# Attention with a gated MLP on one core: centred rows for the first gate/up tile by tile, the last transposes between two filler pairs, and the final adds on GpSimd

## The chip, the cores and the metric

One core of one Trainium2 chip. The metric is device time in microseconds (us), median of several executions. TensorE's granted clock in them was 0.999 or 1.0 on average.

## The reference

```python
x  = A_x                                   # 2048 x 512, bf16
xn = _layernorm(x)                         # (x - mean) / sqrt(var + 1e-5), no weight
s  = attention(xn, k_cache, v_cache, wq, wo)   # 32 heads of 128, 2048 keys, output 512 wide
gate, up = xn @ W_gate, xn @ W_up          # 512 -> 1792
y  = ((gate * (gate > 0)) * up) @ W_down   # 1792 -> 512
return x + s * silu(y)
```

The MLP has no bias, and its gate is a ReLU. If a row of xn is written as r·xc, with the centred row xc = x − mean and r = 1/sqrt(var + eps), then gate and up each carry a factor r, ReLU keeps a positive factor, and y carries r². So y can be computed from the centred rows, and r² be put in at the end. This is what the change uses.

## The kernel before

The program runs the MLP in four quarters of 512 rows, then the attention. Three stretches matter.

The head: four row tiles of 128 rows arrive by DMA, are normalized in two pairs, transposed by TensorE and copied to `xnT`. TensorE meanwhile runs 12 + 3 matmuls on zeros (`warm`). They are there for its clock: in the profile they begin 0.43 us apart and, from about 4.2 us on, 0.22 us apart; below, this is called the release of the clock. The first three of the 14 chunks of gate/up then run in two halves of 256 rows.

```python
def head_ln():
    st = ln_stats(0)
    st = ln_stats(1)
    sq01 = ln_aggr([0, 1], st)             # aggregate, then sqrt on ScalarE
    st = ln_stats(2)
    c01 = ln_coef([0, 1], sq01)            # reciprocal, -mean*rstd
    n0 = ln_norm(dve, sem_ln4, 0, c01)
    n1 = ln_norm(dve, sem_ln4, 1, c01)
    head_transpose(0, n0, act, sem_xa)
    head_transpose(1, n1, act, sem_xa)
    warm_mm(3)
    # ... the same for tiles 2 and 3, between
    emit_half(0, range(HFC - 1), xt_ready[0][0:2])   # gate/up, 256 columns
    emit_half(0, range(HFC - 1, HFC), [])
    emit_half(1, range(HFC), xt_ready[0][2:4])
```

Gate/up results go through a ring of three PSUM slots of two banks. A slot is free again once ScalarE's ReLU and VectorE's multiply have read it.

The tail: the last head group's output projection, 16 row tiles. Tiles 0 to 7 run inside the last attention blocks. Tiles 8 to 11 are fillers that TensorE runs while VectorE normalizes the last attention block; then come that block's transposes, then tiles 12 to 15.

```python
def emit_final_tile(n, bank):
    # ... four matmuls into ps_r[:, bank]
    mtok = sem_opa.sig(
        dve.tensor_tensor(fin_tmp[fb][:], ps_r[:, bank, 0:D], g_sb[:, n, :], ALU.mult))
    _wait(dve, mtok)
    ftok = sem_opa.sig(
        dve.tensor_tensor(x_sb[:, n, :], x_sb[:, n, :], fin_tmp[fb][:], ALU.add))
    # ... store: tiles 12 to 15 one by one, the others in pairs

for n in range(NT - 8, NT - 4, 2):
    emit_M([(emit_final_tile, n), (emit_final_tile, n + 1)])
flush_last_transposes()
for n in range(NT - 4, NT, 2):
    emit_M([(emit_final_tile, n), (emit_final_tile, n + 1)])
```

The softmax here doesn't subtract the row's maximum and nothing guards it: scores larger than these inputs give would overflow.

## Time and profile before

| | before |
|---|---|
| time, median | 1288.09 us (1287.98 to 1288.51) |
| span of the profiled run | 1285.8 us |
| TensorE busy | 1279.2 us |
| first gate/up matmul | 7.80 us |
| last P·V matmul ends (as modelled) | 1274.21 us |
| last add ends | 1283.79 us |

From the page of the kernel before, parts 1 and 4 (busy time with share of the span and number of instructions; the chain that ended last, by engine):

```profile
PE 1279.2 (99%) x11995; PEld 834.8 (65%) x11995; DVE 380.0 (30%) x682; ACT 1001.4 (78%) x1109; POOL 10.0 (1%) x21
...
PE 99%; DVE 1%; issue 0%; DMA 0%; ACT 0%
```

The execution that was profiled took 1287.70 us.

TensorE (PE) bounds everything but two ends. From the timeline of its first 14 us (start, length in us, engine, line, operation; in brackets the idle time before it and what ended it):

```profile
1.19 4.25 PE L365 MATMUL ps_r<-warm 128*128 128x512 bf16 x12 [1.19 <-DVE warm L235]
6.16 0.63 PE L353 MATMUL ps_acc<-ident,xn_sb 128*128 128x128 bf16 x8 [0.71 <-DVE xn_sb L340]
...
7.80 0.60 PE L407 MATMUL ps_r<-xnT,Wg_sb 128*128 128x256 bf16 x4 [0.36 <-ACT xnT L359]
...
13.48 1.03 PE L481 MATMUL ps_r<-xnT,Wg_sb 128*128 128x512 bf16 x4
```

From 7.80 us on no bracket stands any more: TensorE is fed without a gap. The other end, from the timeline of the last 14 us:

```profile
1274.04 3.62 PE L759 MATMUL ps_r<-Wo_sb,OT_store 128*128 128x512 bf16 x16
...
1278.33 3.61 PE L759 MATMUL ps_r<-Wo_sb,OT_store 128*128 128x512 bf16 x16 [0.44 <-ACT OT_store L699]
...
1275.21 0.68 DVE L767 TENSOR_TENSOR fin_tmp<-ps_r,g_sb 128x512 bf16<-128x512 f32 x1
1275.93 0.42 DVE L772 TENSOR_TENSOR x_sb<-x_sb,fin_tmp 128x512 bf16<-128x512 bf16 x1
...
1282.64 0.68 DVE L767 TENSOR_TENSOR fin_tmp<-ps_r,g_sb 128x512 bf16<-128x512 f32 x1
1283.36 0.43 DVE L772 TENSOR_TENSOR x_sb<-x_sb,fin_tmp 128x512 bf16<-128x512 bf16 x1
```

VectorE works through eight tiles at (1282.64 − 1275.21)/7 = 1.06 us each, without a gap between 1275.21 and 1283.79, and is 2 us behind TensorE at the end.

### The profile page before, as it was taken

The numbers are of one execution on the slowest core, as the hardware profiler recorded it, in microseconds if no ns is written. First come the engines' busy times: TensorE is split into PE (matmuls) and PEld (weight loads), VectorE is DVE, ScalarE is ACT, GpSimd is POOL, SyncE is SP. The second block draws the span as 40 slices with busy tenths as digits, with TensorE's granted clock in tenths as the row PEclk, the third lists the DMA queues.
The fourth block names the chain that finished last, engine by engine and source line by source line (L and its number), as shares of the span: only waits on it lengthen the run. The fifth ranks groups of instructions, "written<-read, shape, count | busy, mean of one in ns | idle before, by whom it ended". The sixth has DMA issues, their size and how long they took to land.

```text
span 1285.8 us, 26847 instructions
## 1 busy us (share of the span) xinstructions
PE 1279.2 (99%) x11995; PEld 834.8 (65%) x11995; DVE 380.0 (30%) x682; ACT 1001.4 (78%) x1109; POOL 10.0 (1%) x21
## 2 busy tenths in 40 slices
PE   9999999999999999999999999999999999999998
PEld 4444476666666666666666666666666666666665
DVE  6333311112222222222222222222222222234456
ACT  3322399998888888888888888888888888888884
POOL 2000000000000000000000000000000000000000
PEclk9999999999999999999999999999999999999999
DMA  9500123232222332232322322332223321233302
GB/s 266 111 1 1 21 36 67 57 54 40 36 51 50 71 54 50 54 71 51 54 46 37 60 47 53 55 67 55 54 51 71 55 34 38 50 67 55 50 14 74
DMA packets 238801, 71.60 MB, mean 56 GB/s; under 512 B 225632, under 2 KB 238688, under 8 KB 238688
## 3 DMA queue, kind: packets, MB, share of 16 engines
q1 hardware_dynamic: 238400, 69.63, 27.8%
q8 instruction: 96, 1.57, 0.5%
q10 hardware_dynamic: 288, 0.26, 0.1%
q14 instruction: 17, 0.14, 0.0%
HBM read 32.77 MB, written 2.10 MB: 27 GB/s over the span
## 4 chain that ended last, share of the span: by engine, by line
PE 99%; DVE 1%; issue 0%; DMA 0%; ACT 0%
PE ps_acc L722 36%; PE ps_r L625 34%; PE ps_r L558 9%; PE ps_r L579 8%; PE ps_acc L504 4%; PE ps_r L485 4%; PE ps_r L481 4%; PE ps_r L759 1%; DVE fin_tmp L767 0%; PE ps_r L407 0%; DMA x_sb<-in_A_x_dram 0%; DVE stats L315 0%; ACT xnT L359 0%; PE ps_acc L353 0%; DVE x_sb L772 0%
## 5 line engine op out<-in xcount | busy, mean ns | idle before, releaser
L635 ACT ACTIVATE PT<-ps_r 128x1024 bf16<-128x1024 f32 x1024 | 952.5, 1054 | 167.7 <-PE ps_r L625 167.7
L722 PEld LDWEIGHTS ps_acc<-V_sb,PT 128*128 128x128 bf16 x8192 | 621.1, 98 | 241.7 <-ACT PT L635 3.5
L722 PE MATMUL ps_acc<-V_sb,PT 128*128 128x129 bf16 x8192 | 776.5, 220 | 0.0
L625 PE MATMUL ps_r<-QT_sb,KT_sb 128*128 128x512 bf16 x2048 | 754.1, 379 | 0.0
L652 DVE RECIPROCAL rz_sb<-ps_acc 128x4 f32<-128x4 f32 x127 | 23.3, 183 | 729.6 <-PE ps_acc L722 729.6
L625 PEld LDWEIGHTS ps_r<-QT_sb,KT_sb 128*128 128x128 bf16 x2048 | 195.0, 98 | 1.1 <-DVE QT_sb L569 0.4
L558 PE MATMUL ps_r<-xnT,Wq_sb 128*128 128x512 bf16 x512 | 130.9, 379 | 0.0
L579 PE MATMUL ps_r<-Wo_sb,OT_store 128*128 128x512 bf16 x448 | 114.6, 379 | 0.0
L569 DVE CAST QT_sb<-ps_r 128x512 bf16<-128x512 f32 x128 | 88.5, 692 | 48.1 <-PE ps_r L558 48.1
L558 PEld LDWEIGHTS ps_r<-xnT,Wq_sb 128*128 128x128 bf16 x512 | 49.9, 97 | 60.7 <-ACT PT L635 27.1
L655 DVE TENSOR_TENSOR Onorm<-ps_acc,rz_sb 128x512 bf16<-128x512 f32 x127 | 87.8, 691 | 4.4
L579 PEld LDWEIGHTS ps_r<-Wo_sb,OT_store 128*128 128x128 bf16 x448 | 43.8, 98 | 52.9 <-ACT PT L635 0.2
L448 ACT ACTIVATE gr_sb<-ps_r 128x512 bf16<-128x512 f32 x56 | 33.3, 596 | 51.5 <-PE ps_r L481 49.9
L592 DVE TENSOR_TENSOR s_acc<-s_acc,ps_r 128x512 f32<-128x512 f32 x96 | 66.0, 687 | 17.3 <-PE ps_r L579 17.3
L485 PE MATMUL ps_r<-xnT,Wu_sb 128*128 128x512 bf16 x212 | 54.4, 379 | 0.0
L481 PE MATMUL ps_r<-xnT,Wg_sb 128*128 128x512 bf16 x212 | 54.4, 379 | 0.0
L454 DVE TENSOR_TENSOR hT<-gr_sb,ps_r 128x512 bf16<-128x512 bf16 x56 | 38.4, 686 | 46.3 <-PE ps_r L485 42.0
L504 PE MATMUL ps_acc<-Wd_sb,hT 128*128 128x512 bf16 x224 | 49.0, 379 | 0.0
L510 ACT ACTIVATE sig_sb<-ps_acc 128x512 f32<-128x512 f32 x16 | 9.6, 597 | 38.8 <-PE ps_acc L504 38.8
L504 PEld LDWEIGHTS ps_acc<-Wd_sb,hT 128*128 128x128 bf16 x224 | 21.9, 98 | 26.4
L485 PEld LDWEIGHTS ps_r<-xnT,Wu_sb 128*128 128x128 bf16 x212 | 20.7, 98 | 25.0
L481 PEld LDWEIGHTS ps_r<-xnT,Wg_sb 128*128 128x128 bf16 x212 | 20.8, 98 | 24.8
(42 smaller groups left out, 138.7 us busy)
## 6 DMA issues: line engine op xcount, KB each, us to landing
V_sb<-in_A_v_cache_dram SPq DMA_DIRECT2D x32, 512.0 KB, 4.5
Wq_sb<-in_A_wq_dram SPq DMA_DIRECT2D x32, 128.0 KB, 2.4
Wo_sb<-in_A_wo_dram SPq DMA_DIRECT2D x8, 512.0 KB, 3.9
OT_store<-Onorm SPq DMA_TRANSPOSE x127, 2.4
Wd_sb<-in_B_W_down_dram SPq DMA_DIRECT2D x1, 1792.0 KB, 13.6
x_sb<-in_A_x_dram SPq DMA_DIRECT2D x3, 512.0 KB, 10.1
out_dram<-x_sb SPq DMA_DIRECT2D x6, 256.0 KB, 2.2
Wg_sb<-in_B_W_gate_dram SPq DMA_DIRECT2D x1, 768.0 KB, 9.8
```

The costliest lines, as they stand in the source:

```text
L454: dve.tensor_tensor(hT[par][:, fc, :], gr_sb[gk][:], ps_r[:, gb + 1, :], ALU.mult)
L481: ins = pe.matmul(ps_r[:, gb, :], Wg_sb[:, c, fs], xnT[:, c, qs], start=(c == 0), stop=(c == DC - 1))
L485: ins = pe.matmul(ps_r[:, gb + 1, :], Wu_sb[:, c, fs], xnT[:, c, qs], start=(c == 0), stop=(c == DC - 1))
L504: ins = pe.matmul(ps_acc[:, jb, 0:D], hT[par][:, fc, j * 128:(j + 1) * 128], Wd_sb[:, fc, :], start=(fc == 0), stop=(fc == FC - 1))
L558: ins = pe.matmul(ps_r[:, bank, :], Wq_sb[b][:, c, :], xnT[:, c, qs], start=(c == 0), stop=(c == DC - 1))
L569: etok = sem_qpe.sig(dve.tensor_copy(QT_sb[b][:, qs], ps_r[:, bank, :]))
L579: ins = pe.matmul(ps_r[:, bank, 0:D], OT_store[g % 2][:, hh, n * 128:(n + 1) * 128], Wo_sb[g % 2][:, hh, :], start=(hh == 0), stop=(hh == ...
L592: dve.tensor_tensor(s_acc[:, n, :], s_acc[:, n, :], ps_r[:, bank, 0:D], ALU.add)
L625: ins = pe.matmul(ps_r[:, 2 * s + tt, :], KT_sb[h % 2][:, t * 128:(t + 1) * 128], QT_sb[h % 2][:, qs], start=True, stop=True)
L635: act.activation(PT[pb][:], ps_r[:, 2 * s:2 * s + 2, :], ACTF.Exp, scale=scale)
L655: dve.tensor_tensor(Onorm[ob][:], o_ap, rz_sb[:].to_broadcast([128, 4, Dh]), ALU.mult))
L722: ins = pe.matmul(o_ap, PT[pb][:, tt, j * 128:(j + 1) * 128], V_sb[vb][:, t, 0:VW], start=(t == 0 and j % 2 == 0), stop=(t == KT - 1 and j ...
```

## The change

The intent has two parts. Head: start the first gate/up matmuls on centred rows, tile by tile, so that no square root, reciprocal or partner tile stands in front; issue the first weights earlier and on two queues; put r² into the first quarter's SiLU. Tail: run the last transposes after the first filler pair, so that TensorE does not wait for their copies; let GpSimd do the final adds except the last, so that VectorE has only the multiply.

```diff
                 load_x0(sp, 0)
                 load_x0(act, 1)
+                load_w(sp, Wg_sb, wg_src, sem_wg, 0)
+                load_w(act, Wu_sb, wu_src, sem_wu, 0)
                 load_x0(sp, 2)
                 load_x0(act, 3)
-                load_w(sp, Wg_sb, wg_src, sem_wg, 0)
-                load_w(sp, Wu_sb, wu_src, sem_wu, 0)
@@ head, new
+                def head_center(n):
+                    atok = ln_aggr([n], ln_stats(n))
+                    _wait(dve, atok)
+                    return sem_ln4.sig(
+                        dve.tensor_scalar(xc_sb[:, n, :], x_sb[:, n, :], mv[:, n, 0:1], None, op0=ALU.subtract))
                 def head_ln():
+                    ctok = {0: head_transpose(0, head_center(0))}
+                    warm_mm(2)
+                    for n in range(4):
+                        if n + 1 < 4:
+                            ntok = head_center(n + 1)
+                        _wait(pe, ctok[n])
+                        head_tile(n, 0)                    # chunk 0, 128 columns
+                        if n + 1 < 4:
+                            ctok[n + 1] = head_transpose(n + 1, ntok)
+                        for fc in range(1, HFC):
+                            head_tile(n, fc)
@@ cut: the first quarter's norm moves to GpSimd and a DMA transpose, for the Q projection;
@@ its down stage gets r2 (tanh scale, one more VectorE pass per tile)
-                warm_mm(12)
+                warm_mm(10)
@@ tail
-                fin_tmp = [S_([128, D], BF16, "fin_tmp") for _ in range(2)]
+                fin_tmp = [S_([128, D], BF16, "fin_tmp") for _ in range(4)]
-                    _wait(dve, mtok)
+                    eng, sem = (dve, sem_opa) if n == NT - 1 else (pool, sem_xp)
+                    _wait(eng, mtok)
-                    ftok = sem_opa.sig(
-                        dve.tensor_tensor(x_sb[:, n, :], x_sb[:, n, :], fin_tmp[fb][:], ALU.add))
+                    ftok = sem.sig(
+                        eng.tensor_tensor(x_sb[:, n, :], x_sb[:, n, :], fin_tmp[fb][:], ALU.add))
                 for n in range(NT - 8, NT - 4, 2):
                     emit_M([(emit_final_tile, n), (emit_final_tile, n + 1)])
-                flush_last_transposes()
+                    if n == NT - 8:
+                        flush_last_transposes()
```

More of the change, by code (lines that the diff above doesn't have):

```diff
@@ L141, in bass_recurrent_scan__mha_block_cached__glu_gated_reglu__prompt_kernel @@
         xn_sb = SB_([128, NT, D], BF16, "xn_sb")
+        xc_sb = SB_([128, 4, D], BF16, "xc_sb")
+        xcT = SB_([128, DC, NQ], BF16, "xcT")
+        r2 = SB_([128, 4, 1], F32, "r2")
+        r2h = SB_([128, 4, 1], F32, "r2h")
         stats = SB_([128, NT, 6], F32, "stats")
@@ L320, in ln_aggr, with ln_sqrt @@
                         atok = sem_ln2.sig(dve.bn_aggr(mv[:, n, :], stats[:, n, :]))
+                    return atok
+                def ln_sqrt(ns, atok):
                     a, b_ = ns[0], ns[-1] + 1
                     _wait(act, atok)
-                    if a == 0:
-                        _wait(act, warm_tok)
                     return sem_sq.sig(
@@ L343, in _, with head_transpose @@
                 xt_ready = {Q: [] for Q in range(QB)}
-                def head_transpose(n, ntok, eng, sem):
+                def head_center(n):
[3 more added lines that the diff above has]
+                        dve.tensor_scalar(xc_sb[:, n, :], x_sb[:, n, :], mv[:, n, 0:1], None, op0=ALU.subtract))
+                def head_transpose(n, ntok):
                     tp_ps = acc_bf[n % 2]
@@ L353, in head_transpose @@
                         ins = pe.transpose(tp_ps[:, c * 128:(c + 1) * 128],
-                                           xn_sb[:, n, c * 128:(c + 1) * 128], ident[:])
+                                           xc_sb[:, n, c * 128:(c + 1) * 128], ident[:])
                     ptok = sem_tp.sig(ins)
                     src = tp_ps[:, 0:DC * 128].rearrange("p (c q) -> p c q", c=DC)
-                    _wait(eng, ptok)
-                    copy = act.copy if eng is act else dve.tensor_copy
-                    ctok = sem.sig(copy(xnT[:, :, n * 128:(n + 1) * 128], src))
-                    xt_ready[0].append(ctok)
-                    acc_free[n % 2] = ctok
+                    _wait(act, ptok)
+                    acc_free[n % 2] = sem_xa.sig(act.copy(xcT[:, :, n * 128:(n + 1) * 128], src))
+                    return acc_free[n % 2]
                 def warm_mm(k):
@@ L367, in head_ln @@
                 def head_ln():
-                    st = ln_stats(0)
-                    st = ln_stats(1)
-                    sq01 = ln_aggr([0, 1], st)
-                    st = ln_stats(2)
-                    c01 = ln_coef([0, 1], sq01)
-                    n0 = ln_norm(dve, sem_ln4, 0, c01)
-                    n1 = ln_norm(dve, sem_ln4, 1, c01)
-                    head_transpose(0, n0, act, sem_xa)
-                    head_transpose(1, n1, act, sem_xa)
-                    warm_mm(3)
-                    st = ln_stats(3)
@@ L379, in head_ln @@
-                    sq23 = ln_aggr([2, 3], st)
-                    emit_half(0, range(HFC - 1), xt_ready[0][0:2])
-                    c23 = ln_coef([2, 3], sq23)
-                    n2 = ln_norm(dve, sem_ln4, 2, c23)
-                    n3 = ln_norm(dve, sem_ln4, 3, c23)
-                    head_transpose(2, n2, act, sem_xa)
-                    head_transpose(3, n3, dve, sem_xt)
-                    emit_half(0, range(HFC - 1, HFC), [])
-                    emit_half(1, range(HFC), xt_ready[0][2:4])
@@ L389, in _ @@
-                half_slots = []
-                def emit_half(k, fcs, toks):
-                    hs = slice(k * 256, (k + 1) * 256)
-                    for fc in fcs:
-                        fs = slice(fc * 128, (fc + 1) * 128)
-                        if k == 0:
-                            if fc == 0:
-                                pe.wait_ge(sem_wg[0].h, 16)
-                            half_slots.append(ring_acquire())
-                        if fc == 0:
-                            _wait_all(pe, toks)
-                        s = half_slots[fc]
-                        for i, W in enumerate((Wg_sb, Wu_sb)):
-                            if k == 0 and fc == 0 and i == 1:
-                                pe.wait_ge(sem_wu[0].h, 16)
-                            ins = None
-                            for c in range(DC):
-                                ins = pe.matmul(ps_r[:, 2 * s + i, hs], W[:, c, fs], xnT[:, c, hs],
-                                                start=(c == 0), stop=(c == DC - 1))
-                            if k == 1:
-                                half_tok[(fc, i)] = (sem_gate if i == 0 else sem_gu).sig(ins)
+                    ctok = {0: head_transpose(0, head_center(0))}
@@ new lines, in head_ln, with head_tile @@
+                    warm_mm(2)
[8 more added lines that the diff above has]
+                            head_tile(n, fc)
+                half_slots = []
+                def head_tile(n, fc):
+                    hs = slice(n * 128, (n + 1) * 128)
+                    fs = slice(fc * 128, (fc + 1) * 128)
+                    if n == 0:
+                        half_slots.append(ring_acquire())
+                    s = half_slots[fc]
+                    for i, (W, sems) in enumerate(((Wg_sb, sem_wg), (Wu_sb, sem_wu))):
+                        if n == 0 and fc == 0:
+                            pe.wait_ge(sems[0].h, 16)
+                        ins = None
+                        for c in range(DC):
+                            ins = pe.matmul(ps_r[:, 2 * s + i, hs], W[:, c, fs], xcT[:, c, hs],
+                                            start=(c == 0), stop=(c == DC - 1))
+                        if n == 3:
+                            half_tok[(fc, i)] = (sem_gate if i == 0 else sem_gu).sig(ins)
@@ L412, in _, with ln_finish @@
                 half_tok = {}
                 ln_hold = {}
+                def ln_finish(Q):
+                    ns, sqtok = ln_hold.pop("sq")
+                    ctok = ln_coef(ns, sqtok)
+                    for n in ns:
+                        ntok = ln_norm(pool, sem_nm, n, ctok)
+                        _wait(sp, ntok)
+                        xt_tok = sem_xq[Q].sig(
+                            sp.dma_start_transpose(xnT[:, :, n * 128:(n + 1) * 128], xn_sb[:, n, :]))
+                    xt_ready[Q] = [xt_tok]
+                    return ctok
@@ L416, in ln_task @@
                 def ln_task(i):
                     if i < 4 * (QB - 1):
-                        n = 4 + i
-                        ln_hold["st"] = ln_stats(n)
-                    if i % 4 == 3 and 4 + i < NT:
-                        Q = 1 + i // 4
-                        ns = list(range(4 * Q, 4 * Q + 4))
-                        ln_hold["sq"] = (ns, ln_aggr(ns, ln_hold["st"]))
-                    elif "sq" in ln_hold:
-                        ns, sqtok = ln_hold.pop("sq")
-                        ctok = ln_coef(ns, sqtok)
-                        for n in ns:
-                            ntok = ln_norm(pool, sem_nm, n, ctok)
-                            _wait(sp, ntok)
-                            Q = n // 4
-                            xt_tok = sem_xq[Q].sig(
-                                sp.dma_start_transpose(xnT[:, :, n * 128:(n + 1) * 128], xn_sb[:, n, :]))
-                        xt_ready[Q] = [xt_tok]
-                        if Q == QB - 1:
-                            issue_first()
+                        ln_hold["st"] = ln_stats(4 + i)
@@ new lines, in ln_task @@
+                        if i % 4 == 3:
+                            ns = list(range(i + 1, i + 5))
+                            ln_hold["sq"] = (ns, ln_sqrt(ns, ln_aggr(ns, ln_hold["st"])))
+                        elif i >= 4 and i % 4 == 0:
+                            ln_finish(i // 4)
+                    elif i == 4 * (QB - 1):
+                        ln_finish(QB - 1)
+                        issue_first()
+                        ns = list(range(4))
+                        ln_hold["sq"] = (ns, ln_sqrt(ns, sem_ln2.cur()))
+                    elif i == 4 * (QB - 1) + 1:
+                        ctok = ln_finish(0)
+                        _wait(dve, ctok)
+                        rtok = sem_ln3.sig(dve.tensor_tensor(r2[:], rstd[:, 0:4, :], rstd[:, 0:4, :], ALU.mult))
+                        _wait(dve, rtok)
+                        ln_hold["r2"] = sem_ln3.sig(
+                            dve.tensor_scalar(r2h[:], r2[:], 0.5, None, op0=ALU.mult))
@@ L474, in emit_gate_up @@
                             _wait_all(pe, xt_ready[Q])
+                        xT, xs = (xcT, slice(0, NQ)) if Q == 0 else (xnT, qs)
                         if Q == 0 and fc in FCS:
@@ L480, in emit_gate_up @@
                         for c in range(DC):
-                            ins = pe.matmul(ps_r[:, gb, :], Wg_sb[:, c, fs], xnT[:, c, qs],
+                            ins = pe.matmul(ps_r[:, gb, :], Wg_sb[:, c, fs], xT[:, c, xs],
                                             start=(c == 0), stop=(c == DC - 1))
@@ L484, in emit_gate_up @@
                         for c in range(DC):
-                            ins = pe.matmul(ps_r[:, gb + 1, :], Wu_sb[:, c, fs], xnT[:, c, qs],
+                            ins = pe.matmul(ps_r[:, gb + 1, :], Wu_sb[:, c, fs], xT[:, c, xs],
                                             start=(c == 0), stop=(c == DC - 1))
@@ L508, in emit_down @@
                         _wait(act, sig_free[jb])
+                        if Q == 0 and j == 0:
+                            _wait(act, ln_hold["r2"])
                         stok = sem_sig.sig(
-                            act.activation(sig_sb[jb][:], ps_acc[:, jb, 0:D], ACTF.Tanh, scale=0.5))
+                            act.activation(sig_sb[jb][:], ps_acc[:, jb, 0:D], ACTF.Tanh,
+                                           scale=r2h[:, j, 0:1] if Q == 0 else 0.5))
                         _wait(dve, stok)
-                        gtok = sem_g.sig(
-                            dve.scalar_tensor_tensor(g_sb[:, n, :], sig_sb[jb][:], 1.0, ps_acc[:, jb, 0:D],
-                                                     op0=ALU.add, op1=ALU.mult))
+                        if Q == 0:
+                            ttok = sem_g.sig(
+                                dve.tensor_scalar(sig_sb[jb][:], sig_sb[jb][:], 1.0, r2[:, j, 0:1],
+                                                  op0=ALU.add, op1=ALU.mult))
+                            _wait(dve, ttok)
+                            gtok = sem_g.sig(
+                                dve.tensor_tensor(g_sb[:, n, :], sig_sb[jb][:], ps_acc[:, jb, 0:D], ALU.mult))
+                        else:
+                            gtok = sem_g.sig(
+                                dve.scalar_tensor_tensor(g_sb[:, n, :], sig_sb[jb][:], 1.0, ps_acc[:, jb, 0:D],
+                                                         op0=ALU.add, op1=ALU.mult))
                         y_bank_free[jb] = gtok
@@ L518, in emit_down @@
                     hT_free[par] = ytok
-                assert DC == 4 and FC >= 4 * (QB - 1) + 1
+                assert DC == 4 and QB >= 2 and FC >= 4 * (QB - 1) + 2
                 _wait(pe, warm_w)
-                warm_mm(12)
+                warm_mm(10)
                 head_ln()
@@ L555, in emit_qp @@
                     _wait(pe, wq_tok(h))
+                    if h == 0 and Q == 0:
+                        _wait_all(pe, xt_ready[0])
                     ins = None
@@ L767, in emit_final_tile @@
                         dve.tensor_tensor(fin_tmp[fb][:], ps_r[:, bank, 0:D], g_sb[:, n, :], ALU.mult))
-                    _wait(dve, mtok)
+                    eng, sem = (dve, sem_opa) if n == NT - 1 else (pool, sem_xp)
+                    _wait(eng, mtok)
                     if n == 0:
-                        _wait(dve, base_done[NT - 1])
-                    ftok = sem_opa.sig(
-                        dve.tensor_tensor(x_sb[:, n, :], x_sb[:, n, :], fin_tmp[fb][:], ALU.add))
+                        _wait(eng, base_done[NT - 1])
+                    ftok = sem.sig(
+                        eng.tensor_tensor(x_sb[:, n, :], x_sb[:, n, :], fin_tmp[fb][:], ALU.add))
                     fin_free[fb] = ftok
```

## The prediction

> **What bounds the kernel now.** TensorE. The page shows PE busy 1279.2 of 1285.8 us, and the chain of waits is 99% PE. The timeline has PE without a gap from 7.80 us (first gate/up matmul) to 1277.9 us. Only two stretches are not PE-bound: the head up to 7.80 us, and the tail after the last P·V matmul (1274.1 us), where the timeline shows VectorE working alone: eight pairs of a 0.69 us multiply and a 0.42 us add, one tile per 1.06 us, from 1275.21 to 1283.79, then about 2.0 us for the last store. The change touches only these two; it cannot move the time by more than about 3 us (0.25%).
>
> **Head.** Removed: square root, reciprocal, coefficients and the wait for a pair of tiles before the first transpose. Centring alone: row statistics 0.68, aggregate 0.16, subtract 0.41 us after x lands at 3.13, so the first centred tile is there at about 4.45 instead of 6.0. Ten warm matmuls end near 5.0; transposes and a 0.58 us copy put the activations ready at about 6.0. But the first weights then bound: the DMA view has them landing at 6.25 and 7.7 us; issued 0.45 and 0.9 us earlier, I estimate both near 6.4. So the stream starts near 6.4 instead of 7.80: 1.4 us.
> Given back: 96 matmuls of 128 columns at about 56 ns (the 129-column ones run at 57 ns) against 48 at 109 ns, 0.1 us; one more tile's transposes inside the stream, 0.22 us; and a new wait: the last tile's sweep over the three chunks lasts only 1.35 us, while the first chunk's slot is freed by a 0.60 us ReLU and 0.69 us multiply after it, so the fourth chunk waits about 0.45 us. Head: about 0.6 us gained (0 to 1).
>
> Later additions are off the path: the first quarter's norms on GpSimd (0.77 us each) and their transposes finish long before the Q projection at 141 us; the extra 0.4 us VectorE pass in its down stage fits in 3.0 us per tile.
>
> **Tail.** Transposes after the first filler pair remove PE's 0.44 us wait; the last output tile leaves PE near 1281.4 instead of 1281.9. VectorE keeps only the multiplies and ends near 1282.6 with the last add. But seven adds go to GpSimd. This trace has no two-input GpSimd operation; its one-input 128x512 takes 0.77 us. The Trainium skill, "GPSIMD Engine Reference" section 3.1, measures 2.6 cycles per element for a two-input add: my estimate from that page is 1.1 us for 512 elements. Then GpSimd, not VectorE, ends last: 1275.95 + 7 x 1.1 = 1283.7, plus an issue of the last two stores in a row: about 0.4 us lost. At 0.9 us or less, about 1.2 us would be gained. Weighed: about 0 gained.
>
> **Prediction.** 1287.5 us, 8 in 10 between 1286.3 and 1288.7. Faster by over 2%: 0.002; within 2%: 0.996; slower: 0.002.
>
> **What would show it.** Right: first gate/up matmul between 6.1 and 6.9, waiting for a weight DMA, not the copy; a gap of about 0.4 us on PE before the first 512-column gate matmul; that one starting near 12.9 (was 13.48); no PE gap between there and the tail; GpSimd adds of about 1.1 us back to back ending after VectorE's last add. Wrong: adds under 0.9 us; weights landing after 7 us because two queues interleave; a gap before the third tile's transposes because its x now queues behind weights.
>
> **What would make it wrong.** GpSimd's add time above all (each 0.1 us is 0.7 us at the end), then the weights' landing.

## The result

| | before | changed |
|---|---|---|
| time, median of 6 | 1288.03 us (1287.91 to 1288.51) | 1288.15 us (1287.68 to 1289.59) |
| span of the profiled run | 1285.8 us | 1286.4 us |
| first gate/up matmul | 7.80 us | 6.74 us |
| last P·V matmul ends | 1274.21 us | 1274.09 us |
| last add ends | 1283.79 us (VectorE) | 1283.84 us (GpSimd) |
| from the last add to the end of the span | 2.0 us | 2.5 us (before rounding the span) |

The ratio is 1.0002, interval 0.9989 to 1.0015. A ratio is the mean time of one kernel's fast runs over that of the other's of the same rounds, so it is not quite the ratio of the medians. The kernel before is the steadier one.

The profile of the changed kernel, parts 1 and 4:

```profile
PE 1279.5 (99%) x12040; PEld 835.5 (65%) x12040; DVE 377.0 (29%) x670; ACT 1001.8 (78%) x1109; POOL 30.3 (2%) x40
...
PE 99%; POOL 1%; DVE 0%; ACT 0%; POOLq 0%; issue 0%; DVEq 0%
```

The 1% of the chain that was VectorE's is now GpSimd's (POOL). Its head, from the timeline of TensorE (the last line was asked for with a window to 14.5 us):

```profile
1.19 4.45 PE L374 MATMUL ps_r<-warm 128*128 128x512 bf16 x10 [1.19 <-DVE warm L239]
...
6.74 0.40 PE L402 MATMUL ps_r<-xcT,Wg_sb 128*128 128x128 bf16 x4 [0.15 <-ACT xcT L369]
...
13.36 1.02 PE L488 MATMUL ps_r<-xcT,Wg_sb 128*128 128x512 bf16 x4 [0.42 <-ACT gr_sb L454]
```

The first gate/up matmul starts 1.06 us sooner than before, the first 512-column one only 0.12 us sooner, and a new wait of 0.42 us stands in front of it: for the ReLU (`gr_sb`) of the first chunk, which has to free the ring slot. The weights' landing, from the DMA view (KB each, us from issue to landing):

```profile
Wu_sb<-in_B_W_up_dram ACTq DMA_DIRECT2D x1, 384.0 KB, 4.9
Wg_sb<-in_B_W_gate_dram SPq DMA_DIRECT2D x1, 384.0 KB, 4.4
```

They were issued at 1.17 and 1.18 us, so they landed at 6.1 and 5.6 us. The tail, from the timeline of GpSimd and VectorE:

```profile
1275.09 1.45 DVE L787 TENSOR_TENSOR fin_tmp<-ps_r,g_sb 128x512 bf16<-128x512 f32 x2
1275.85 7.99 POOL L793 TENSOR_TENSOR x_sb<-x_sb,fin_tmp 128x512 bf16<-128x512 bf16 x7 [1.37 <-DVE fin_tmp L787]
...
1281.25 0.69 DVE L787 TENSOR_TENSOR fin_tmp<-ps_r,g_sb 128x512 bf16<-128x512 f32 x1 [0.17 <-PE ps_r L779]
1281.98 0.85 DVE L793 TENSOR_TENSOR x_sb<-x_sb,fin_tmp 128x512 bf16<-128x512 bf16 x1
```

GpSimd runs seven adds back to back. With a window from 1282.6 to 1284 us, the last one stands alone:

```profile
1282.51 1.33 POOL L793 TENSOR_TENSOR x_sb<-x_sb,fin_tmp 128x512 bf16<-128x512 bf16 x1
```

So six adds start (1282.51 − 1275.85)/6 = 1.11 us apart, against VectorE's 1.06 us for multiply and add together; each of the six has 1.15 us in the record. The last one has 1.33 us: it starts while VectorE's own last add is running (1281.98 to 1282.83 us). VectorE now waits 0.17 us for TensorE before each of the last multiplies, that is, it keeps pace with TensorE, but GpSimd falls behind and ends at 1275.85 + 7.99 = 1283.84 us, just where VectorE ended before. The store of tile 14, which waits for it, is then issued in front of the store of tile 15, whose add was done at 1282.83 us.

### The profile page after: what moved, and what is told of

It reads as the page before. It is cut to its first block, busy times and chain, and to the rows that moved or that the text cites. A ratio compares the mean times of both kernels' runs of the same rounds, so it can differ in the third digit from the quotient of the medians.

```text
span 1286.4 us, 26946 instructions
## 1 busy us (share of the span) xinstructions
PE 1279.5 (99%) x12040; PEld 835.5 (65%) x12040; DVE 377.0 (29%) x670; ACT 1001.8 (78%) x1109; POOL 30.3 (2%) x40
## 4 chain that ended last, share of the span: by engine, by line
PE 99%; POOL 1%; DVE 0%; ACT 0%; POOLq 0%; issue 0%; DVEq 0%
PE ps_acc L742 36%; PE ps_r L645 34%; PE ps_r L578 9%; PE ps_r L599 8%; PE ps_acc L511 4%; PE ps_r L488 4%; PE ps_r L492 4%; PE ps_r L779 1%; POOL x_sb L793 1%; PE ps_r L374 0%; PE ps_r L402 0%; PE ps_acc L364 0%; POOLq L202 0%; ACT gr_sb L454 0%; DVE fin_tmp L787 0%
## 5 line engine op out<-in xcount | busy, mean ns | idle before, releaser
L793 POOL TENSOR_TENSOR x_sb<-x_sb,fin_tmp 128x512 bf16<-128x512 bf16 x15 | 17.1, 1165 | 1227.7 <-DVE fin_tmp L787 1227.7
L488 PE MATMUL ps_r<-xnT,Wg_sb 128*128 128x512 bf16 x168 | 43.1, 379 | 0.0
L492 PE MATMUL ps_r<-xnT,Wu_sb 128*128 128x512 bf16 x168 | 43.1, 379 | 0.0
L492 PEld LDWEIGHTS ps_r<-xnT,Wu_sb 128*128 128x128 bf16 x168 | 16.4, 98 | 19.8
```

Of the source, the lines that this page charges most:

```text
L488: ins = pe.matmul(ps_r[:, gb, :], Wg_sb[:, c, fs], xT[:, c, xs], start=(c == 0), stop=(c == DC - 1))
L492: ins = pe.matmul(ps_r[:, gb + 1, :], Wu_sb[:, c, fs], xT[:, c, xs], start=(c == 0), stop=(c == DC - 1))
```

## The experiments

My theory after the result was that the head gained little in this execution and that the tail lost: GpSimd's add is longer than VectorE's whole tile, and two stores then stand in a row. The rivals were that the head had gained the predicted 0.6 us and the tail lost all of it; or that the tail was neutral and the head was to blame. Each time is compared with the runs of the kernel before on the same chip. In all that follows, the distance "from the last P·V matmul to the last add" separates the tail from the head, and the end of the last P·V matmul (1274.21 us in the profile of before) shows what the head and the middle did; the middle did not change (the middle from 158.4 to 1270 us has TensorE busy for all of its 1111.60 us in both kernels).

### head_only and tail_only

`head_only` is the changed kernel with the tail of before; `tail_only` is the kernel before with the changed tail. The diff is that of the change, cut at the line "@@ tail".

> Only the head of the change on the old tail. Theory (the head gained almost nothing, the tail lost about what it gained): the first 512-column gate matmul starts near 13.4 us (before 13.48, the whole change 13.36), the tail is as before with the last VectorE add about 9.7 us after the last P.V matmul, the time is 0.1 us under before, within 0.3 us. Rival 1 (the head gained the 0.6 us that was predicted and the tail lost all of it): 0.5 us or more under before. Rival 2 (the larger spread of the changed kernel's runs comes from the tail): its spread over rounds stays within 0.6 us; if it comes from the head, the spread is 1 us or more.

> Only the tail of the change on the old head. Theory: seven GpSimd adds of 1.14 us back to back end the arithmetic at about the same distance from the last P.V matmul as VectorE did, and two stores issued one after the other then add 0.5 us: 0.5 to 0.7 us over before. Rival (the tail is neutral, the head lost): within 0.2 us of before.

| | time, median of 5 | range | before, same chip | last P·V matmul ends | from there to the last add | last add to end |
|---|---|---|---|---|---|---|
| head_only | 1287.58 | 1286.93 to 1287.68 | 1288.04 (1287.94 to 1288.11) | 1273.43 | 9.58 | 2.0 |
| tail_only | 1288.77 | 1288.58 to 1288.94 | 1288.04 (1287.94 to 1288.11) | 1274.65 | 9.76 | 2.5 |
| before (profile) | | | | 1274.21 | 9.58 | 2.0 |

The head alone gains 0.46 us of the median and 0.64 us of the mean; all five of its runs lie under all nine of before. The tail alone loses 0.73 us; all five lie over all nine. So my theory of the head was wrong and the first rival right (it asked for 0.5 us or more, which the median just misses and the mean meets): the head brings about the 0.5 to 0.6 us that was predicted, and the tail takes it back. The rival on the tail (neutral) fell as well. The question about the spread stays open: head_only's is 0.75 us, between the two marks, and tail_only's is 0.36 us. Which part of the head's edit brings its gain (centred rows, earlier weights on two queues, or fewer warm matmuls) no run separates.

The tail of tail_only, from its timeline:

```profile
1272.67 1.98 PE L722 MATMUL ps_acc<-V_sb,PT 128*128 128x129 bf16 x32
...
1276.41 8.00 POOL L773 TENSOR_TENSOR x_sb<-x_sb,fin_tmp 128x512 bf16<-128x512 bf16 x7 [1.37 <-DVE fin_tmp L767]
```

In the tail's 0.7 us, about 0.2 us are arithmetic (9.76 against 9.58) and 0.5 us are the time after the last add. The 0.2 us are just what the last GpSimd add takes more than the others, here too 1.33 against 1.15 us: it meets VectorE's last add.

The last P·V matmul ended at 1274.21 and 1274.65 us in the two profiled runs of the old head. It ended between 1273.41 and 1274.72 us, 1273.94 on average, in the seven profiled runs of the new head with its 10 warm matmuls and its order. One profile is not the head's size: the changed kernel's own (1274.09) showed only 0.1 us of its gain, also because the profile of before is an early one. In the old head, the 0.44 us between the two profiles come from the first rows of x: VectorE's first statistics began at 3.15 us in before and at 3.60 us in tail_only, each time after a wait for x. In the new head, part of the scatter is TensorE's clock. The 512-column warm matmuls are 0.43 us apart until it is released. In `head_only` the release came at about 4.1 us; in the changed kernel the spacing was still 0.43 us at 5.4 us, so that the ten stood in front of the transposes for longer.

### adds_on_dve

The changed kernel, all adds on VectorE, the transposes still between the filler pairs.

```diff
-                    eng, sem = (dve, sem_opa) if n == NT - 1 else (pool, sem_xp)
+                    eng, sem = (dve, sem_opa)
```

> The whole change, but all final adds stay on VectorE; the last transposes still run between the two filler pairs. Theory: VectorE bounds the tail again at 1.06 us per tile, the earlier transposes only let TensorE finish 0.6 us earlier with no effect, the last add ends as in before, one store is left: 0.1 to 0.3 us under before and 0.5 us under the whole change. Rival (the earlier transposes are worth their 0.4 us of removed TensorE wait): 0.5 us or more under before.

It took 1287.28 us (1286.81 to 1287.49), 0.76 us under before. That is more than the 0.1 to 0.3 us expected, because the head is in it, which I had put at 0.1 us. By its time alone the rival's mark (0.5 us or more) was met, and it is 0.30 us under head_only by median, with ranges that overlap. The distances in the tail decide: from the last P·V matmul to the last add it took 9.56 us, against 9.58 before, and 2.0 us remained after it. So the earlier transposes are worth nothing that the trace shows as long as VectorE needs 1.06 us per tile, although TensorE's 0.44 us wait is gone; and undoing the move to GpSimd brings back the 0.7 us (9.56 + 2.0 us after the last P·V matmul, against 9.76 + 2.5 in tail_only).

### adds_split

The adds of tiles 9, 12, 14 and 15 on VectorE, the others on GpSimd (a store of two tiles then waits for both engines).

```diff
-                    eng, sem = (dve, sem_opa) if n == NT - 1 else (pool, sem_xp)
+                    eng, sem = (dve, sem_opa) if n in (9, 12, 14, 15) else (pool, sem_xp)
```

> The whole change, with the adds of tiles 9, 12, 14 and 15 on VectorE and of 8, 10, 11 and 13 on GpSimd. If the two engines do not hinder each other (theory A): GpSimd is done near 1281.7 us, VectorE near 1282.8, the span ends near 1284.9, 1.0 to 1.4 us under before. If an add on VectorE cannot run while GpSimd's add runs, as the 0.85 us of the single VectorE add beside a running GpSimd add suggests, against 0.42 us alone (theory B): the VectorE adds of tiles 9, 12 and 14 each last 0.8 us or more, the multiplies behind them slip, and the span ends at 1285.5 us or later.

It took 1287.43 us (1286.82 to 1287.75), no better than all adds on VectorE. From its timeline:

```profile
1275.53 1.16 POOL L794 TENSOR_TENSOR x_sb<-x_sb,fin_tmp 128x512 bf16<-128x512 bf16 x1 [1.37 <-DVE fin_tmp L788]
1276.25 0.71 DVE L794 TENSOR_TENSOR x_sb<-x_sb,fin_tmp 128x512 bf16<-128x512 bf16 x1
...
1277.64 2.26 POOL L794 TENSOR_TENSOR x_sb<-x_sb,fin_tmp 128x512 bf16<-128x512 bf16 x2 [0.96 <-DVE fin_tmp L788]
...
1279.06 1.12 DVE L794 TENSOR_TENSOR x_sb<-x_sb,fin_tmp 128x512 bf16<-128x512 bf16 x1
...
1280.87 1.15 POOL L794 TENSOR_TENSOR x_sb<-x_sb,fin_tmp 128x512 bf16<-128x512 bf16 x1 [0.96 <-DVE fin_tmp L788]
1281.42 0.88 DVE L794 TENSOR_TENSOR x_sb<-x_sb,fin_tmp 128x512 bf16<-128x512 bf16 x1
...
1282.93 0.43 DVE L794 TENSOR_TENSOR x_sb<-x_sb,fin_tmp 128x512 bf16<-128x512 bf16 x1
```

The VectorE add with no GpSimd add beside it takes 0.43 us; the three that start while one runs take 0.71, 1.12 and 0.88 us. Each of these ends 0.27 or 0.28 us after the GpSimd add that it overlaps (1276.96 after 1276.69, 1280.18 after 1279.90, 1282.30 after 1282.02). The Trainium skill says in "SBUF — State Buffer", section "Who interferes with whom", that a VectorE instruction with two SBUF inputs contends with a GpSimd instruction that reads SBUF, and that whichever issues second is blocked. This trace agrees, and the multiplies, which have only one SBUF input, keep their 0.69 us beside a GpSimd add, as the page also says. So theory B holds in its mechanism (one of the three adds, 0.71 us, is shorter than the 0.8 us expected, because GpSimd was further on; and the span ended at 1285.4 us, just short of the 1285.5 expected): sharing the adds out between these two engines gains nothing here, 9.60 us from the last P·V matmul to the last add against 9.56 with all of them on VectorE. The same wait is the 0.85 us of the changed kernel's last VectorE add, which ends 0.28 us after the sixth GpSimd add (1282.83 after 1282.55), and the other order is there too: the seventh GpSimd add, which starts while that VectorE add runs, takes 1.33 us instead of 1.15.

### store_act

The changed kernel; the last tile's store is issued by ScalarE.

```diff
-                        _wait(sp, ftok)
-                        sem_out.sig(sp.dma_start(out_t[:, n0:n + 1, :], x_sb[:, n0:n + 1, :]))
+                        q = act if n == NT - 1 else sp
+                        _wait(q, ftok)
+                        sem_out.sig(q.dma_start(out_t[:, n0:n + 1, :], x_sb[:, n0:n + 1, :]))
```

> The whole change, with the store of the last tile issued by ScalarE instead of by SyncE behind the store of the tile before it. Theory (the second of two stores in a row costs its issue and its turn): the GpSimd adds still end last, the span ends about 0.4 us sooner after them than in the whole change (about 2.1 instead of 2.5 us after the last add), 0.2 to 0.4 us under before. Rival (the last stores are bound by the transfer, not by the issue): no change from the whole change, within 0.15 us of the same distance from the last add to the end.

The last add, GpSimd's, again ended 9.75 us after the last P·V matmul, and the span ended about 2.0 us after it instead of about 2.5 (before rounding, the spans are 1285.88 and 1286.36 us). The time was 1287.67 us (1287.41 to 1288.62), 0.28 us under before (1287.95 us on this chip). The half microsecond after the last add was the second store's turn on SyncE, not the transfer. The distance shows this and the time does not: after_again, below, is the changed kernel unaltered and was 0.31 us under before.

### warm7

As adds_on_dve, with 7 instead of 10 warm matmuls before the first transposes.

```diff
-                warm_mm(10)
+                warm_mm(7)
```

> All adds on VectorE, and 7 instead of 10 warm matmuls before the first transposes. Theory (the warm matmuls that run at the slow clock stand in front of the first transposes; the weights, landed at 5.6 and 6.1 us, do not bound): transposes at 4.9 to 5.0 us, first gate/up matmul at 5.9 to 6.2 us in every run, a smaller spread, 0.2 us under the 1287.3 us of the same kernel with 10. Rival (the pause that this opens in front of the transposes delays the release of the TensorE clock): 128-column matmuls at about 107 instead of 56 ns for part of the stream, first 512-column gate matmul after 13.3 us, slower by 0.3 us or more than with 10.

It took 1287.17 us (1286.61 to 1287.62), 0.78 us under before, where adds_on_dve was 0.76 us under. In the profile the transposes ran at 4.88 us and the first gate/up matmul at 6.14 us, as expected, and the 128-column matmuls were 56 ns apart, so the rival did not show. But the third tile's transposes, at 8.43 us, came 0.27 us late, since their x had landed only at 7.0 us; it queues behind the weights now. The earlier start was partly lost again, and the spread of the runs did not fall (1.01 us, against 0.68 us in adds_on_dve). This run moves the time by less than it can show.

### fc_order

As adds_on_dve, with the head's last two tiles in another order; the fourth tile's transposes also come one step sooner, and all centring is issued before the first chunk.

```diff
-                    for n in range(4):
-                        ...
+                    order = [(0, 0), "T1", (0, 1), (0, 2), (1, 0), "T2", (1, 1), (1, 2), "T3",
+                             (2, 0), (2, 1), (3, 0), (3, 1), (2, 2), (3, 2)]   # (tile, chunk), Tn: transposes
```

> All adds on VectorE, and the last two tiles of the head in another order, chunks 0 and 1 of tile 2, then chunks 0 and 1 of tile 3, then chunk 2 of both, so that chunk 0 is finished 0.45 us sooner before the fourth chunk wants its slot. Theory (the gap of 0.4 to 0.6 us on TensorE before the first 512-column gate matmul is the wait for the first chunk's ReLU and multiply): the gap falls to 0.2 us or less, that matmul starts 6.4 us or less after the first gate/up matmul (6.6 to 7.0 in the four runs of this head), 0.3 to 0.5 us under the 1287.3 us. Rival (the gap is the wait for the second group of weights): the gap stays.

Its timeline, where the first 512-column gate matmuls start:

```profile
13.21 0.81 PE L490 MATMUL ps_r<-xcT,Wg_sb 128*128 128x512 bf16 x3 [0.18 <-issue]
```

The same line of act_evac, the next experiment, which has the old order and in whose profile the first gate/up matmul also started at 6.74 us:

```profile
13.57 0.81 PE L489 MATMUL ps_r<-xcT,Wg_sb 128*128 128x512 bf16 x3 [0.63 <-ACT gr_sb L455]
```

Both lines hold three of the group's four matmuls. The record of the first is missing, and a matmul is 0.216 us, so the true gaps are about 0 and 0.42 us. The gap is the slot's wait for the first chunk, as predicted, and not the weights. Like against like, the line starts 0.36 us sooner. The time, 1287.04 us (1286.85 to 1287.29), is 0.91 us under before, 0.15 us better than adds_on_dve was on its chip; the expected 0.3 to 0.5 us were not reached there.

### act_evac

As adds_on_dve; for the last eight tiles ScalarE first copies the sum to a bf16 buffer.

```diff
+                    src, rtok = ps_r[:, bank, 0:D], otok
+                    if n >= NT - 8:
+                        _wait(act, otok)
+                        _wait(act, fin_free[fb])
+                        src, rtok = fin_ev[fb][:], sem_exp2.sig(act.copy(fin_ev[fb][:], ps_r[:, bank, 0:D]))
-                        dve.tensor_tensor(fin_tmp[fb][:], ps_r[:, bank, 0:D], g_sb[:, n, :], ALU.mult))
+                        dve.tensor_tensor(fin_tmp[fb][:], src, g_sb[:, n, :], ALU.mult))
@@ cut: VectorE waits for rtok; the PSUM bank is handed back after the copy; adds on VectorE
```

> All adds on VectorE, and for the last eight tiles ScalarE, idle there, first copies the sum from PSUM to a bf16 buffer, so that VectorE's multiply has two bf16 operands in SBUF. Theory (VectorE's 1.06 us per tile bound the tail, and the multiply takes 0.69 us because it reads f32 from PSUM): multiply 0.42 us, 0.85 us per tile, the tail then follows TensorE's 0.86 us per tile, the last add ends 0.5 us sooner, 0.4 to 0.6 us under the 1287.3 us. Rival (the multiply stays at 0.69 us, or the extra step adds its latency): no gain or a loss.

The chain of waits of its last microseconds, in order of time:

```profile
1276.03 5.19 PE ps_r L781 x24
1281.22 0.02 issue
1281.24 0.59 ACT fin_ev L790
1281.84 0.02 issue
1281.86 0.44 DVE fin_tmp L794
1282.30 0.02 issue
1282.32 0.42 DVE x_sb L801
```

One of VectorE's multiplies, from the timeline:

```profile
1280.13 0.42 DVE L794 TENSOR_TENSOR fin_tmp<-fin_ev,g_sb 128x512 bf16<-128x512 bf16 x1
```

The multiply fell from 0.69 to 0.42 us, and TensorE itself now stands in the chain until 1281.22 us. The last add ended 8.66 us after the last P·V matmul instead of 9.56. Since TensorE now bounds, its 0.44 us wait would count here, and so the earlier place of the transposes should be of use; this is argued and not shown, since no run has the copy with the transposes in their old place. The time is 1286.61 us (1286.58 to 1286.79), 1.34 us under before, and the result is still correct against the reference.

### combined10, combined7 and after_again

`combined10` joins fc_order and act_evac; `combined7` has 7 warm matmuls besides; `after_again` is the changed kernel as it is.

> The two edits that helped, together: the other order of the head's last two tiles, and ScalarE's copy ahead of VectorE's multiply for the last eight tiles, all adds on VectorE, 10 warm matmuls. If the two ends of the kernel add up: 0.4 us (fc_order's gap) less than act_evac's 1286.6 us, 1286.2 to 1286.5, which is 1.5 to 1.8 us under before. If not: 1286.6 or more.

> The same with 7 warm matmuls. In a run whose clock is released late the first gate/up matmul starts 0.6 us sooner (6.14 against 6.74 us), but the third tile's transposes then wait for its x, which landed at 7.0 us there, so half of that is lost again: 0 to 0.3 us under combined10. Rival: the pause delays the clock in some runs, and the spread is 1 us or more.

> The changed kernel as it is, once more, beside the others on one chip. Head and tail measured alone were 0.5 us under and 0.7 us over before; if they add up, it is 0.1 to 0.4 us over before, with a spread of 1 us or less; the 1289.59 us of its first runs is then a rare one.

| | time, median of 5 | range | ratio to before, 95% interval |
|---|---|---|---|
| combined10 | 1286.23 | 1285.75 to 1286.61 | 0.9986, 0.9974 to 0.9999 |
| combined7 | 1285.99 | 1285.57 to 1288.06 | 0.9989, 0.9976 to 1.0001 |
| after_again | 1287.70 | 1287.32 to 1288.83 | 0.9998, 0.9984 to 1.0011 |
| before, same chip | 1288.01 | 1287.71 to 1288.12 | |

combined10 is 1.78 us under before, as the two ends added up predict, and beats both kernels. combined7 has the lowest median and a spread of 2.5 us, with two of five runs above 1287 us; by means it is the slower of the two. What happened in those two runs no profile shows; that the pause costs the clock there is a guess left open. after_again was 0.31 us under before by median and 0.06 us by mean, where its first six runs were 0.12 and 0.24 us over: around zero, as head and tail together give (−0.64 + 0.74 of the means). What was expected of it was missed in both points: it was to be 0.1 to 0.4 us over before, with a spread of 1 us or less, and its spread was 1.5 us. Its profiled run shows one more source of scatter:

```profile
7.39 0.38 PE L402 MATMUL ps_r<-xcT,Wg_sb 128*128 128x128 bf16 x4 [0.73 <-DMA Wg_sb<-in_B_W_gate_dram]
```

Here the first gate weights landed only at about 7.3 us (6.1 us after the issue, against 4.3 to 4.5 us in the six other profiled runs of this head and order), and the stream waited for them. Smaller waits stand in two other runs, both for the up weights. In adds_on_dve they landed at about 6.3 us, and the first up matmul came 0.36 us after the first gate matmul (5.93 and 6.29 us) instead of the 0.23 us of head_only. In combined7, from its weight loads (PEld):

```profile
6.60 0.23 PEld L405 LDWEIGHTS ps_r<-xcT,Wu_sb 128*128 128x128 bf16 x4 [0.16 <-DMA Wu_sb<-in_B_W_up_dram]
```

## Why the prediction was right, point by point

- The time, 1288.15 us, lies in the predicted range of 1286.3 to 1288.7 us, and within 2% as said. The centre, 1287.5, was 0.65 us too low: the gain of 0.6 us did not come. An unchanged time (1288.09) lies in that range too, so the hit alone says little; the points below say more.
- "Head: about 0.6 us gained" held: −0.46 us by the medians, −0.64 us by the means, with the head alone. That the sum fits so well owes something to luck, since terms under it came out otherwise, as the next point says.
- Its inner steps held in part. The wait for the fourth chunk (predicted about 0.45 us, measured 0.42) held, and fc_order removed it; the matmul behind it was to start near 12.9 us and started at 13.36. "But the first weights then bound" failed in the profiled run: they landed at 5.6 and 6.1 us, and what stood in front was the warm matmuls, all ten of which ran at 0.43 us spacing, then transposes and copy; the stream began at 6.74 us instead of 6.4. In other profiled runs of this head the weights did bound: by 0.73 us in after_again (start at 7.39 us), by about 0.1 us in adds_on_dve. "Ten warm matmuls end near 5.0" is true only in the runs with an early clock. And "x lands at 3.13" was read from an execution in which x came early: in the changed kernel the first statistics began at 3.49 us.
- The gap before the third tile's transposes was named as a risk. It did not show in the changed kernel; it showed in warm7 (0.27 us), where the stream began early.
- Tail: "my estimate … is 1.1 us" for GpSimd's add held: 1.11 us from start to start, and GpSimd ended last, at 1283.84 us (predicted 1283.7). The skill's figure of 2.6 cycles per element ("GPSIMD Engine Reference", section 3.1), measured there on f32, carried over to bf16 here.
- The step that was mis-sized is the last one of the tail: "about 0.4 us lost", then "Weighed: about 0 gained". Measured with the tail alone, it lost 0.73 us: about 0.2 us because the last adds of the two engines met, which the prediction did not have, and 0.5 us of a second store in a row. The weighing put nearly half of the chance on an add of 0.9 us or less, against the one source that had a figure. With the tail's own estimate unweighed, the sum would have been +0.4 − 0.6 = −0.2, or 1287.9 us.
- "Transposes after the first filler pair remove PE's 0.44 us wait" was right and worth nothing that the traces show, since VectorE bounded (adds_on_dve); in act_evac TensorE bounds, and it should count there, which no run tested.

## What to carry to other kernels

Before work is moved to a slower engine to relieve a faster one, compare the moved operation with the whole period that it is to beat: here one add on GpSimd (1.11 us from start to start) was longer than multiply and add together on VectorE (1.06 us), so the tail changed its engine and not its length. Look then for an idle engine beside which the busy one keeps its times: a copy by ScalarE made VectorE's own multiply cheaper (0.69 to 0.42 us), VectorE's adds beside it kept their 0.42 to 0.43 us, and it brought what the move was meant to bring. Where both ends of a kernel are changed at once, time each end alone: two true effects of 0.6 and 0.7 us cancelled here and looked like no effect at all.

## What the Trainium skill lacked or had wrong

- "GPSIMD Engine Reference", section 3.1, gives a two-input add only for f32 with 2048 elements; for bf16 and 512 elements the runs show 1.11 us from start to start and 1.15 us in the record of one add.
- "SBUF — State Buffer", section "Who interferes with whom", gives the rule and no number for a VectorE add behind a GpSimd add; here it ended 0.27 to 0.28 us after the GpSimd add, 0.43 us being its length alone. The other way round, a GpSimd add that started behind a VectorE add took 1.33 us instead of 1.15.
- "DMA: Bandwidth & Descriptors", section "Issuing engines are not separate DMA queues", calls the sequencer time saved by issuing from a second engine "usually small relative to the DMA itself"; for the last of two stores in a row at the end of the kernel it was 0.5 us (about 2.5 to 2.0 us after the last add), beside about 1.7 us from the issue of such a store to its landing.
- "TensorE: Matmul & The Clock Gate", part 1, puts the clock's release at about 4 us of sustained activity, give or take 0.5 us. TensorE's activity begins at 1.19 us in these runs, and the slow spacing of its matmuls ended at about 4.1 us in head_only, which is 2.9 us later, but only at about 6.9 us in fc_order, 5.7 us later (four gate matmuls in a row there still took 0.31 us from 6.74 us on, against 0.22 us for the next four). This scatter is wider than the 0.5 us, though a note in the same part does warn that the count of slow matmuls varies from run to run.
- No page says that single matmul records can be missing from a profile: two of the lines shown hold three of four matmuls, which made a gap of 0.42 us read as 0.63.
